# Row maxima of windowed attention in tiles of 64 queries of two heads by 320 keys

## The chip, the core and the metric

One Trainium2 chip, one core. The metric is device time in microseconds of one execution of the whole kernel. Engines are called PE (TensorE, matrix multiply; PEld is its weight load), DVE (VectorE), ACT (ScalarE), POOL (GpSimd) and SP (SyncE, which here only issues DMAs).

## What is computed

A transformer layer over 2048 tokens of width 512: layer norm, attention with 32 heads of 16 in a causal window of 256, a residual, a second layer norm, and a mixture of 8 experts of which each token takes two. The part that the change touches:

```python
scores = jnp.einsum("bhqd,bhkd->bhqk", q, k) * (Dh ** -0.5)
mask = (idx[:, None] - idx[None, :] >= 0) & (idx[:, None] - idx[None, :] < W)   # W = 256
scores = jnp.where(mask[None, None], scores, -1e9)
p = _softmax(scores, axis=-1)
o = jnp.einsum("bhqk,bhkd->bhqd", p, v)
```

## The kernel before

The tokens are worked in 4 chunks of 512 (`c`), the heads in 8 groups of 4 (`g`); a chunk and a group make a unit, 32 in all. `qk` (L583) projects Q and K of a unit in high and low halves of float32 (three matmuls for one product), writes them to DRAM (`qkd`) and reads them back into a slot of SBUF, of which there are four (`Q[i]`, `K[i]`, L263 to L266). In a slot, K holds two heads above each other: 48 rows from partition 0 are the 16 dimensions of an even head in three parts, 48 rows from partition 64 those of an odd head; its columns are 768 keys, 256 before the chunk and 512 of it. Q holds for each head only that head's rows; the others stay zero from a memset at the start (L477), so a matmul of a head's Q with the pair's K sees that head alone. `rq` (L631) and `rk` (L635) are the loads, one of each for the even heads and one for the odd ones; `rq` moves rows of 512 floats.

`maxes` (L647) finds each query's largest score. For a block of 128 queries and a head, one matmul (L666) has 128 queries as its weights and 384 keys as its moving operand; DVE adds a mask of the window to it and reduces it to the maximum in one instruction (L671, `tensor_tensor_reduce`, which the trace shows as CUSTOM_DVE_ANT_0 and a read of its accumulator). That is 16 matmuls and 16 reductions a unit. In chunk 0, where no keys lie before the first, blocks 0 and 1 have 128 and 256 keys, and several heads share a PSUM bank. At most three banks hold maxima (pool `mx`). `fin` (L677) negates and splits the maxima, a DMA writes them to DRAM (`md`, L684), and another (L687) reads them into rows 126 and 127 of the slot's Q, where K has ones. So the score matmuls of `attend` (L713), which have keys as weights and queries as moving operand, already subtract the maximum. ACT takes the exponential (L717), POOL clears what lies outside the window (L737), and PE multiplies by V (L758).

The order on every engine is made ahead by a planner: each step is given to `add` with an engine, a duration in ns and a priority, and `Plan.order` (L126) simulates them with pools of buffers (`one`: 7 PSUM banks; `qk`: 4 slots); a table `SHIFT` (L41) moves priorities of kinds of steps in spans of eight units. The engines then run exactly that order, and wait for each other by semaphores. Durations for a matmul are `n * 0.4355 + 8` (L215), for a reduction `110 + n * 1.041` (L675). From about 500 us on the experts run (`up` L1259, `down` L1290, `down_32` L1330).

## Time and profile before

| | us |
|---|---|
| median of 3 runs | 1072.37 |
| lowest and highest | 1070.73, 1073.33 |
| the profiled execution, device time | 1069.08 |
| its span in the trace | 1067.3 |

The page of the profile gives busy time by engine, the share of DMA engines, and groups of instructions by line. A busy PE counts from a matmul's start to its modelled end, and matmuls overlap, so the time that a matmul takes is read from the starts of a dense run of them. The granted clock of PE is 1.00, 2.4 GHz, in every stretch of attention.

### The profile page before, as it was taken

The page shows a single profiled execution, that of the slowest core. Times are in us where ns is not written, and L with a number is a line of the kernel's source. Part 1 is how long each engine was busy: PE and PEld are TensorE (multiplying, and loading weights), DVE is VectorE, ACT ScalarE, POOL GpSimd, SP SyncE. Part 2 cuts the span into 40 slices and gives each one's busy share as a digit, 9 for nine tenths or more (in the row PEclk, how much of TensorE's full clock was granted, in tenths as well). Part 3 has the DMA queues.
Part 4 walks back from the last instruction along what each step waited for, and adds up shares of the span by engine and source line. Part 5 has one row for each costly group of instructions (what it writes and reads, how often), then busy time and mean ns, then how long its engine had stood idle before and what let it go on. Part 6 is the DMA issues. An engine that isn't in the chain of part 4 may idle for free.

```text
span 1067.3 us, 19631 instructions
## 1 busy us (share of the span) xinstructions
PE 1037.5 (97%) x6722; PEld 862.7 (81%) x6722; DVE 673.9 (63%) x1834; ACT 540.0 (51%) x1139; POOL 610.8 (57%) x922
## 2 busy tenths in 40 slices
PE   9999999999999999998999999999999999999993
PEld 6777777877788777755889898999989998788893
DVE  9988888888787787884742645444564445645331
ACT  3376667565655766567624452552643624445230
POOL 6575569676786767688683161472853737542101
PEclk9999999999999999999999999999999999999997
DMA  7988978777784786864513644344634546354411
GB/s 248 235 250 214 227 194 247 194 178 197 188 246 125 170 244 168 237 182 148 174 43 97 160 126 112 84 105 116 154 94 100 126 123 151 99 143 133 109 35 26
DMA packets 102082, 165.57 MB, mean 155 GB/s; under 512 B 26052, under 2 KB 38404, under 8 KB 101972
## 3 DMA queue, kind: packets, MB, share of 16 engines
q1 hardware_dynamic: 87892, 146.48, 49.1%
q0 software_dynamic: 14080, 17.74, 9.8%
q8 instruction: 55, 0.90, 0.4%
q14 instruction: 55, 0.45, 0.1%
HBM read 111.91 MB, written 52.26 MB: 154 GB/s over the span
## 4 chain that ended last, share of the span: by engine, by line
PE 83%; DMA 5%; DVE 5%; POOL 3%; issue 1%; ACT 1%; SPq 1%; POOLq 0%; ACTq 0%; DVEq 0%
PE one L1259 24%; PE one L1290 15%; PE one L713 8%; PE one L666 8%; PE one L1330 7%; PE oT L758 7%; PE one L607 5%; PE one L836 3%; PE one L551 2%; PE one L927 1%; DVE one L671 1%; DMA mf<-in_A_wqk_dram 1%; DMA mf<-xnd,tb 1%; DMA mr<-md 1%; DMA mf<-in_A_x_dram 1%
## 5 line engine op out<-in xcount | busy, mean ns | idle before, releaser
L671 DVE CUSTOM_DVE_ANT_0 one<-one,masked 128x384 f32<-128x384 f32 (+2 forms) x512 | 260.7, 555 | 47.5 <-PE one L666 45.1
L1259 PE MATMUL one<-mr 128*128 128x288 f32 (+8 forms) x1716 | 266.4, 316 | 0.7 <-ACT mr L426 0.7
L1259 PEld LDWEIGHTS one<-mr 128*128 128x128 f32 (+1 forms) x1716 | 249.7, 186 | 12.9 <-ACT mr L426 0.9
L717 ACT ACTIVATE zone<-one 128x384 f32<-128x384 f32 (+1 forms) x480 | 207.0, 499 | 92.9 <-PE one L713 77.9
L737 POOL TENSOR_SCALAR_AFFINE_SELECT zone<-zone 128x256 f32<-128x256 f32 (+1 forms) x368 | 169.3, 483 | 90.4 <-ACT zone L717 88.6
L1290 PE MATMUL one<-zone,mr 128*128 128x512 f32 (+1 forms) x648 | 155.6, 396 | 0.0
L666 PE MATMUL one<-mr 126*128 126x384 f32 (+2 forms) x512 | 152.7, 350 | 1.7 <-DVE mx L671 1.7
L713 PE MATMUL one<-mr 128*128 128x384 f32 (+1 forms) x592 | 143.4, 316 | 2.7 <-DMA mr<-md 1.6
L1290 PEld LDWEIGHTS one<-zone,mr 128*128 128x128 f32 (+1 forms) x648 | 120.5, 187 | 29.0
L428 DVE TENSOR_TENSOR mr<-one,mr 128x512 fp32r<-128x512 f32 (+9 forms) x161 | 83.0, 526 | 89.3 <-ACT mr L426 89.0
L1311 POOL DMA_INDIRECT out_dram<-mf,tb x24 | 39.5, 1645 | 164.3 <-DVE mf L1301 153.3
L1198 POOL DMA_INDIRECT mf<-xnd,mf x97 | 103.2, 1063 | 43.9 <-issue 27.7
L430 POOL TENSOR_TENSOR mr<-mf,mr 128x512 fp32r<-128x512 f32 (+4 forms) x92 | 114.2, 1254 | 23.0 <-ACT mr L426 17.6
L426 ACT CAST mr<-mf 128x512 fp32r<-128x512 f32 (+6 forms) x148 | 108.9, 754 | 29.6 <-DMA mf<-in_A_wqk_dram 16.7
L666 PEld LDWEIGHTS one<-mr 126*128 126x128 f32 x512 | 89.5, 189 | 40.3 <-DVE mx L671 17.1
L1273 ACT ACTIVATE one<-one 128x288 f32<-128x288 f32 (+7 forms) x132 | 56.5, 428 | 128.1 <-PE one L1259 127.8
L713 PEld LDWEIGHTS one<-mr 128*128 128x128 f32 x592 | 102.1, 189 | 22.9 <-ACT zone L717 7.1
L1311 POOL DMA_INDIRECT out_dram<-mf x40 | 64.2, 1605 | 72.4 <-DVE mf L1340 62.8
L607 PE MATMUL one<-mr 128*128 128x512 f32 (+1 forms) x396 | 102.1, 387 | 0.9 <-DVE mx L671 0.9
L758 PE MATMUL oT<-zone 128*17 128x384 f32 (+2 forms) x1408 | 96.0, 387 | 2.4 <-POOL zone L737 2.4
L426 ACT CAST mr<-one 128x512 fp32r<-128x512 f32 (+9 forms) x161 | 73.4, 461 | 32.4 <-PE one L1232 20.2
L607 PEld LDWEIGHTS one<-mr 128*128 128x128 f32 x396 | 70.1, 188 | 11.6 <-DVE mx L671 1.3
(182 smaller groups left out, 1244.4 us busy)
## 6 DMA issues: line engine op xcount, KB each, us to landing
mf<-in_B_w_dram SPq DMA_DIRECT2D x32, 688.0 KB
mf<-in_B_w_dram SPq DMA_DIRECT2D x40, 512.0 KB
mr<-qkd SPq DMA_DIRECT2D x80, 192.0 KB
qkd<-mr SPq DMA_DIRECT2D x29, 512.0 KB
mr<-qkd SPq DMA_DIRECT2D x48, 288.0 KB
mf<-in_A_x_dram SPq DMA_DIRECT2D x32, 256.0 KB
mf<-in_A_wqk_dram SPq DMA_DIRECT2D x32, 256.0 KB
qkd<-mr SPq DMA_DIRECT2D x64, 128.0 KB
```

The costliest lines, as they stand in the source:

```text
L426: a = add("ACT", 51 + n * 0.86, lambda: nc.scalar.copy(dst_h(), src()), deps, prio, bufs)
L430: b = add("POOL", 60 + n * 2.3, lambda: nc.gpsimd.tensor_sub(dst_l(), src(), f32(dst_h())), [a], prio, bufs)
L607: nc.tensor.matmul(single[bk.h][:, s], wt()[:, int(i == 1), k * 128:(k + 1) * 128], xt[:, k, s], start=(i == 0 and k == 0), stop=(i == 2 a ...
L666: nc.tensor.matmul(view()[:, j], Q[slot.h][0:126, h + j, b * 128:(b + 1) * 128], K[slot.h][0:126, (h + j) // 2, (b + k0) * 128:(b + 3) * 1 ...
L671: nc.vector.tensor_tensor_reduce(v, v, masked.rearrange("p a k -> p (a k)")[:, 384 - n:], scale=1.0, scalar=NEG, op0=OP.add, op1=OP.max, a ...
L713: nc.tensor.matmul(single[bk.h][:, off:off + w], K[slot.h][:, h // 2, r * 128:(r + 1) * 128], Q[slot.h][:, h:h + hs, b * 128:(b + m) * 128 ...
L717: return add("ACT", 51 + n * 0.833, lambda: nc.scalar.activation(dst(), single[bk.h][:, 0:n].rearrange(order, q=128, **({"h": 2} if "h" in ...
L737: nc.gpsimd.affine_select(v, v, pattern=[[0, v.shape[1]], [-1 if far else 1, 128]], compare_op=OP.is_gt if far else OP.is_ge, fill=0.0, ba ...
L758: nc.tensor.matmul(oT[32 * j:32 * j + 17, b * 128:(b + n) * 128], V[blk % NV][:, 4 * g + j, :], PT[pt.h][j // 2][:, off:off + n, j % 2], s ...
L1259: nc.tensor.matmul(bank(), a[:, k, f * 128:f * 128 + w], spot[b][:, k, c0:c1], start=(i == 0), stop=(i == 11))
L1290: nc.tensor.matmul(single[bk.h][:n], h[a][:w], spot["w2"][2 * f + b][:w], start=(f == 0 and q == 0), stop=(f == NF - 1 and q == 2))
L1311: d = nc.gpsimd.indirect_dma_start(in_offset=None, compute_op=OP.add, **kw)
```

## The change

A tile of the maxima becomes 64 queries of two heads by 320 keys: the weights are 64 queries of an even head (which are zero in the odd head's rows) and the same 64 of the odd head, so its 128 rows are (head, query); 64 queries look at 64 + 256 keys. Eight blocks and two pairs of heads make 16 tiles a unit, as before. For the weights to lie together, Q is stored as (pair, block of 64, head of the pair, query). The loads of Q write in that layout, 64 floats at a time, and are issued by pair: four of 96 KB a unit in place of two of 192 KB. The score matmuls read Q in runs of 64. The mask is one row of 320 keys, the same in both halves of the partitions. In chunk 0 the first four blocks have 64, 128, 192 and 256 keys. The planner's durations follow from the sizes; `SHIFT` stays, and the names of the steps it speaks of keep their meaning (`rq`, whose name changes, has no entry).

```diff
--- before.py
+++ after.py
@@ -262,7 +262,7 @@
     R2 = at[id(mr)]
     Q, K = [], []
     for i in range(NQ):
-        Q.append(take(mr, 4, 512))
+        Q.append(take(mr, 2048))
         K.append(take(mr, 2, 768))
     R4 = at[id(mr)]
     woh, wol = take(mr, 4, 512), take(mr, 4, 512)
@@ -335,7 +335,7 @@
         return consts.tile(shape, dt, name=name)
 
     ident = const([128, 128], F32, "ident")
-    masked = const([128, 3, 128], BF, "masked")
+    masked = const([128, 320], BF, "masked")
     before = const([128, 128], BF, "before")
     ones = const([128, 128], BF, "ones")
     wgt = const([128, 4, E], F32, "wgt")
@@ -354,8 +354,8 @@
     ry_t = [const([128, 4], F32, f"ry{i}") for i in range(2)]
     v4_t = [const([128, 2], F32, f"v4{i}") for i in range(2)]
     h_t4 = [const([128, 2], F32, f"h4{i}") for i in range(2)]
-    mx_t = [const([128, 4, 4], F32, f"mx{i}") for i in range(NQ)]
-    mm_t = [const([128, 2, 4, 4], F32R, f"mm{i}") for i in range(NQ)]
+    mx_t = [const([128, 2, 8], F32, f"mx{i}") for i in range(NQ)]
+    mm_t = [const([128, 2, 2, 8], F32R, f"mm{i}") for i in range(NQ)]
     mt_t = [const([128, 32], F32, f"mt{i}") for i in range(NQ)]
     mv2_t = [const([128, 2], F32, f"mvh{i}") for i in range(NH)]
     ry2_t = [const([128, 1], F32, f"ryh{i}") for i in range(NH)]
@@ -391,9 +391,10 @@
 
     def consts_first():
 
-        nc.vector.tensor_scalar(masked[:, 0], jp_i, 0, NEG, op0=OP.is_le, op1=OP.mult)
-        nc.vector.memset(masked[:, 1], 0.0)
-        nc.vector.tensor_scalar(masked[:, 2], jp_i, 0, NEG, op0=OP.is_gt, op1=OP.mult)
+        nc.vector.memset(masked[:, 64:256], 0.0)
+        for r in (slice(0, 64), slice(64, 128)):
+            nc.vector.tensor_scalar(masked[r, 0:64], jp_i[r, r], 0, NEG, op0=OP.is_le, op1=OP.mult)
+            nc.vector.tensor_scalar(masked[r, 256:320], jp_i[r, r], 0, NEG, op0=OP.is_gt, op1=OP.mult)
         nc.vector.memset(oT, 0.0)
 
     def consts_dve():
@@ -628,19 +629,23 @@
         slots[u] = slot
         rds = []
         for par in range(2):
-            def rq(par=par):
-                nc.sync.dma_start(f32(Q[slot.h])[par * 64:par * 64 + 48, par::2],
-                                  ap(dd, par * 16 * 3 * S + o, [[S, 48], [32 * 3 * S, 2], [1, 512]]))
+            def rq(pr, par=par):
+                nc.sync.dma_start(f32(q_of(slot))[par * 64:par * 64 + 48, pr, :, par],
+                                  ap(dd, (2 * pr + par) * 16 * 3 * S + o, [[S, 48], [64, 8], [1, 64]]))
 
             def rk(par=par):
                 h = 256 if c else 0
                 nc.sync.dma_start(f32(K[slot.h])[par * 64:par * 64 + 48, :, 256 - h:768],
                                   ap(dd, 64 * 3 * S + S + par * 16 * 3 * S + o - h, [[S, 48], [32 * 3 * S, 2], [1, 512 + h]]))
             dep = wr + [m for k in range(min(u + 1, NQ)) for m in memsets[k]]
-            rds.append(dma(rq, 196608, dep, p + 0.6, [slot]))
+            rds.extend(dma(lambda pr=pr, rq=rq: rq(pr), 98304, dep, p + 0.6, [slot]) for pr in range(2))
             rds.append(dma(rk, 589824, dep, p + 0.6, [slot]))
         qk_read[u] = rds
     slots = {}
+
+    def q_of(slot):
+
+        return Q[slot.h].rearrange("p (a b e q) -> p a b e q", a=2, b=8, e=2)
     m_read = {}
     w_load = []
 
@@ -650,25 +655,25 @@
         slot = slots[u]
         box = {}
         reds = []
-        for b in range(4):
-            k0 = 0 if c else max(0, 2 - b)
-            n = (3 - k0) * 128
-            m = 512 // n
-            for h in range(0, 4, m):
+        for b in range(8):
+            k0 = 0 if c else max(0, 4 - b)
+            n = (5 - k0) * 64
+            m = min(2, 512 // n)
+            for h in range(0, 2, m):
                 bk, lim = Buf("one"), Buf("mx")
-                pp = p + b / 4 + h / 16
+                pp = p + b / 8 + h / 16
 
                 def view(n=n, m=m, bk=bk):
                     return single[bk.h][:, :m * n].rearrange("p (h n) -> p h n", h=m)
 
                 def mm(b=b, h=h, k0=k0, m=m, view=view):
                     for j in range(m):
-                        nc.tensor.matmul(view()[:, j], Q[slot.h][0:126, h + j, b * 128:(b + 1) * 128],
-                                         K[slot.h][0:126, (h + j) // 2, (b + k0) * 128:(b + 3) * 128], start=True, stop=True)
+                        nc.tensor.matmul(view()[:, j], q_of(slot)[0:126, h + j, b].rearrange("p e q -> p (e q)"),
+                                         K[slot.h][0:126, h + j, (b + k0) * 64:(b + 5) * 64], start=True, stop=True)
 
                 def red(j, b=b, h=h, n=n, view=view):
                     v = view()[:, j]
-                    nc.vector.tensor_tensor_reduce(v, v, masked.rearrange("p a k -> p (a k)")[:, 384 - n:], scale=1.0, scalar=NEG,
+                    nc.vector.tensor_tensor_reduce(v, v, masked[:, 320 - n:], scale=1.0, scalar=NEG,
                                                    op0=OP.add, op1=OP.max, accum_out=mx_t[slot.h][:, h + j, b:b + 1])
                 a = add("PE", m * max(107, mm_ns(n)), mm, qk_read[u], pp, [slot, bk, lim])
                 for j in range(m):
@@ -684,7 +689,7 @@
         w = dma(lambda: nc.sync.dma_start(box["d"], mt_t[slot.h]), 30000, [f], p + 1, [slot])
 
         def rd_():
-            nc.sync.dma_start(f32(Q[slot.h])[126:128].rearrange("p h (b i q) -> p (h b) i q", b=4, i=4),
+            nc.sync.dma_start(f32(Q[slot.h])[126:128].rearrange("p (b i q) -> p b i q", i=4, q=32),
                               ap(box["d"], 0, [[512, 2], [32, 16], [1024, 4], [1, 32]]))
         m_read[u] = [dma(rd_, 20000, [w], p + 1.1, [slot], 625)]
 
@@ -711,11 +716,11 @@
                     for r, b, m, h, hs in chunks:
                         w = m * hs * 128
                         nc.tensor.matmul(single[bk.h][:, off:off + w], K[slot.h][:, h // 2, r * 128:(r + 1) * 128],
-                                         Q[slot.h][:, h:h + hs, b * 128:(b + m) * 128], start=True, stop=True)
+                                         q_of(slot)[:, h // 2, 2 * b:2 * b + 2 * m, slice(None) if hs == 2 else h % 2], start=True, stop=True)
                         off += w
                 pe = add("PE", sum(mm_ns(m * hs * 128) + 2 for _, _, m, _, hs in chunks), mm, m_read[u] + qk_read[u], prio, [slot, bk, pt, lim])
                 return add("ACT", 51 + n * 0.833, lambda: nc.scalar.activation(
-                    dst(), single[bk.h][:, 0:n].rearrange(order, q=128, **({"h": 2} if "h" in order else {})), AF.Exp, scale=0.25),
+                    dst(), single[bk.h][:, 0:n].rearrange(order, **({"e": 2, "q": 64} if "e" in order else {"q": 128}), **({"h": 2} if "h" in order else {})), AF.Exp, scale=0.25),
                     [pe], prio, [bk, pt, lim])
 
             for pr in range(2):
@@ -725,7 +730,8 @@
                     k1, k2 = (2, 0) if name == "A" else (0, 1)
                     exps = [scores([(r2, b2, 2, h, 1), (r2, b2, 2, h + 1, 1)],
                                    lambda pt=pt, pr=pr, k2=k2: PT[pt.h][pr][:, k2:k2 + 2].rearrange("p b h q -> p h b q"), "p (h b q) -> p h b q", pp),
-                            scores([(r1, b1, 1, h, 2)], lambda pt=pt, pr=pr, k1=k1: PT[pt.h][pr][:, k1], "p (h q) -> p h q", pp + 1 / 16)]
+                            scores([(r1, b1, 1, h, 2)], lambda pt=pt, pr=pr, k1=k1: PT[pt.h][pr][:, k1].rearrange("p h (e q) -> p h e q", e=2),
+                                   "p (e h q) -> p h e q", pp + 1 / 16)]
                 else:
                     (r, b, _), = parts
                     exps = [scores([(r, b, 3, h + j, 1)], lambda pt=pt, pr=pr, j=j: PT[pt.h][pr][:, :, j], "p (b q) -> p b q", pp + j / 16) for j in range(2)]
```

The first place where the order changes is PE at the start of attention, in chunk 0 (`L607` and `L608` are the projection of Q and K, `L551` and `L552` that of V, `L666` and `L671` the maxima). Before:

```order
L551 MATMUL one_77<-mr 128x512 x4
L666 MATMUL one_78<-mr 128x128 x4
L666 MATMUL one_79<-mr 128x256 x2
L666 MATMUL one_80<-mr 128x256 x2
L607 MATMUL one_74<-mr 128x512 x8
L666 MATMUL one_75<-mr 128x384
L607 MATMUL one_74<-mr 128x512 x4
L666 MATMUL one_76<-mr 128x384
```

and now:

```order
L552 MATMUL one_77<-mr 128x512 x4
L608 MATMUL one_78<-mr 128x512 x4
L671 MATMUL one_79<-mr 128x64 x2
L671 MATMUL one_80<-mr 128x128 x2
L671 MATMUL one_74<-mr 128x192 x2
L608 MATMUL one_78<-mr 128x512 x4
L671 MATMUL one_75<-mr 128x256 x2
L608 MATMUL one_78<-mr 128x512 x4
L671 MATMUL one_76<-mr 128x320
L671 MATMUL one_79<-mr 128x320
```

The maxima of unit 0 now come one burst of the projection later, and in smaller pieces.

The second place is PE in a later chunk, with `L713` and `L718` the score matmuls and `L607` and `L608` the projection of a unit ahead. Before:

```order
L758 MATMUL oT<-zone 17x256 x4
L666 MATMUL one_77<-mr 128x384
L666 MATMUL one_76<-mr 128x384
L713 MATMUL one_74<-mr 128x384
L666 MATMUL one_79<-mr 128x384
L713 MATMUL one_75<-mr 128x384
L713 MATMUL one_80<-mr 128x384
L607 MATMUL one_78<-mr 128x512 x4
L666 MATMUL one_77<-mr 128x384
L666 MATMUL one_74<-mr 128x384
L713 MATMUL one_75<-mr 128x384
```

and now:

```order
L764 MATMUL oT<-zone 17x256 x4
L671 MATMUL one_78<-mr 128x320
L671 MATMUL one_79<-mr 128x320
L718 MATMUL one_80<-mr 128x384
L718 MATMUL one_76<-mr 128x384
L671 MATMUL one_75<-mr 128x320
L718 MATMUL one_74<-mr 128x384
L608 MATMUL one_77<-mr 128x512 x4
L671 MATMUL one_78<-mr 128x320
L671 MATMUL one_80<-mr 128x320
L718 MATMUL one_79<-mr 128x384
```

The mix is the same, one or two maxima to one or two score matmuls, in another rotation of the PSUM banks.

The third is SP's queue in chunk 0, around the maxima of unit 0 (`md` is written at `L684`, now `L689`, and read back at `L687`, now `L692`; `L632`, now `L633`, are loads of Q, `L637`, now `L638`, of K). Before:

```order
L621 DMA qkd_86<-mr 64x512
L622 DMA qkd_86<-mr 64x512
L684 DMA md_544<-mt_136 128x32
L620 DMA qkd_86<-mr 128x2x512
L591 DMA mf<-in_A_wqk_dram 128x512
L632 DMA mr<-qkd_85 48x2x512
L637 DMA mr<-qkd_85 48x2x512
L632 DMA mr<-qkd_85 48x2x512
L687 DMA mr<-md_544 2x64x32
L637 DMA mr<-qkd_85 48x2x512
L621 DMA qkd_87<-mr 64x512
```

and now:

```order
L622 DMA qkd_86<-mr 64x512
L592 DMA mf<-in_A_wqk_dram 128x512
L689 DMA md_551<-mt_136 128x32
L623 DMA qkd_86<-mr 64x512
L621 DMA qkd_86<-mr 128x2x512
L633 DMA mr<-qkd_85 48x8x64 x2
L638 DMA mr<-qkd_85 48x2x512
L692 DMA mr<-md_551 2x64x32
L633 DMA mr<-qkd_85 48x8x64 x2
L638 DMA mr<-qkd_85 48x2x512
```

The read-back has three loads of the next slot ahead of it in both; of the four loads of Q that replace two, two stand ahead of it.

## Rows read from the trace of the kernel before

**Rows 1.** The page, part 1: busy us of each engine, its share of the span, and its instructions.

```profile
PE 1037.5 (97%) x6722; PEld 862.7 (81%) x6722; DVE 673.9 (63%) x1834; ACT 540.0 (51%) x1139; POOL 610.8 (57%) x922
```

**Rows 2.** The page, part 4: the chain that ended last, its share of the span by engine and line.

```profile
PE one L1259 24%; PE one L1290 15%; PE one L713 8%; PE one L666 8%; PE one L1330 7%; PE oT L758 7%; PE one L607 5%; PE one L836 3%; PE one L551 2%; PE one L927 1%; DVE one L671 1%; DMA mf<-in_A_wqk_dram 1%; DMA mf<-xnd,tb 1%; DMA mr<-md 1%; DMA mf<-in_A_x_dram 1%
```

**Rows 3.** Busy time by stretch of the span: the stretch and its length in us, then busy us and number of instructions of PE, PEld, DVE, ACT and POOL, the granted clock, the DMA engines' share and GB/s.

```profile
25.00:75.00 50.00, 47.18 (x274) 37.40 (x273) 46.91 (x172) 25.06 (x53) 32.56 (x43) 1.00 0.93 250
75.00:125.00 50.00, 49.46 (x359) 35.08 (x358) 41.78 (x169) 34.63 (x78) 31.98 (x59) 1.00 0.90 223
125.00:225.00 100.00, 99.06 (x738) 77.42 (x740) 85.62 (x283) 61.35 (x136) 67.56 (x121) 1.00 0.80 206
225.00:325.00 100.00, 99.57 (x745) 78.41 (x734) 79.58 (x246) 61.77 (x138) 75.12 (x133) 1.00 0.78 207
325.00:475.00 150.00, 149.20 (x1153) 111.98 (x1153) 118.21 (x425) 97.99 (x219) 107.34 (x203) 1.00 0.70 185
475.00:555.00 80.00, 74.94 (x462) 58.10 (x462) 45.52 (x118) 44.23 (x98) 65.00 (x102) 1.00 0.39 120
```

**Rows 4.** Instructions of PE in order of time, from three places: attention at 376 us, the first expert at 538 us, a later expert at 726 us. Columns: start in us, length in us to the end of the last one, engine, line, operation, out<-in, shapes, number.

```profile
376.78 0.76 PE L713 MATMUL one<-mr 128*128 128x256 f32 x5
377.38 1.09 PE L607 MATMUL one<-mr 128*128 128x512 f32 x4
378.31 0.51 PE L666 MATMUL one<-mr 126*128 126x384 f32 x2
378.65 0.52 PE L713 MATMUL one<-mr 128*128 128x256 f32 x3
...
538.87 4.43 PE L1259 MATMUL one<-mr 128*128 128x384 f32 x24
543.15 0.18 PE L993 MATMUL one<-r_m,before 128*128 128x16 bf16 x1
...
726.45 4.12 PE L1330 MATMUL one<-mr,zone 128*128 128x320 f32 x27
730.40 1.05 PE L1330 MATMUL one<-mr 128*128 128x320 f32 x6
```

**Rows 5.** The same view of PE in chunk 0, between 40 and 60 us. The first row merges matmuls of 128, 256 and 384 columns and names the shape of the first. In brackets: idle time of the engine before the row, and what ended it.

```profile
40.86 1.08 PE L666 MATMUL one<-mr 126*128 126x128 f32 x8
41.78 2.90 PE L607 MATMUL one<-mr 128*128 128x512 f32 x12
...
53.00 0.76 PE L713 MATMUL one<-mr 128*128 128x384 f32 x3 [1.19 <-DMA mr<-md]
```

**Rows 6.** Groups of instructions by line and shape over the whole span: number, then busy us, mean ns of one, and idle us of the engine before them with what ended it.

```profile
L671 DVE CUSTOM_DVE_ANT_0 one<-one,masked 128x384 f32<-128x384 f32 x448 | 239.2, 582 | 45.4 <-PE one L666 44.1
...
L671 DVE CUSTOM_DVE_ANT_0 one<-one,masked 128x256 f32<-128x256 f32 x32 | 13.7, 446 | 0.5
...
L671 DVE CUSTOM_DVE_ANT_0 one<-one,masked 128x128 f32<-128x128 f32 x32 | 9.5, 297 | 1.6 <-PE one L666 0.9
```

**Rows 7.** Who waited for whom from 0 to 475 us: us in total, times, the longest in us. PEld is PE's weight load.

```profile
PEld one L666 <- DVE mx L671: 16.9, 32, 1.1
...
PEld one L713 <- DVE mx L671: 4.2, 8, 0.6
...
PE one L666 <- DVE mx L671: 1.7, 4, 0.8
```

**Rows 8.** DMA packets of SP's queue (q1) in five stretches, one row each: 132 to 133 us (all 93 packets hold under 512 B; 128 B each by their bytes), 391.5 to 392 us (81 packets under 2 KB; 80 of them of 1 KB), 653.5 to 656.5 us (475 packets, 454 of 2 KB or more), 25 to 125 us, and 125 to 475 us. Columns: packets, MB, share of 16 engines' time in the stretch.

```profile
q1 hardware_dynamic: 93, 0.01, 7.5%
...
q1 hardware_dynamic: 81, 0.08, 45.9%
...
q1 hardware_dynamic: 475, 0.93, 90.5%
...
q1 hardware_dynamic: 15447, 23.51, 91.1%
...
q1 hardware_dynamic: 45267, 68.50, 74.1%
```

**Rows 9.** The chain of waits that ends at 60 us, in order of time: start in us, length in us, what. SPq is SP's issue of a DMA.

```profile
47.10 0.58 SPq L632
...
47.78 5.09 DMA mr<-md
```

**Rows 10.** Two issues of a Q load on SP in order of time, columns as in rows 4.

```profile
22.67 0.37 SPq L632 DMA_DIRECT2D mr<-qkd  x1
...
23.58 0.44 SPq L632 DMA_DIRECT2D mr<-qkd  x1
```

**Rows 11.** DVE's two mask constants, and the first and the last of GpSimd's (POOL) memsets beside them, columns as in rows 4.

```profile
22.13 4.64 DVE L394 TENSOR_SCALAR masked<-mf 128x128 bf16<-128x128 int32 x1
22.22 1.40 POOL L478 MEMSET mr<- 128x1536 f32 x1
...
22.34 4.50 DVE L396 TENSOR_SCALAR masked<-mf 128x128 bf16<-128x128 int32 x1
...
25.30 1.40 POOL L478 MEMSET mr<- 128x1536 f32 x1
```

**Rows 12.** Reductions of DVE in chunk 0 in order of time, the first and the last of six, columns as in rows 4.

```profile
46.37 0.60 DVE L671 CUSTOM_DVE_ANT_0 one<-one,masked 128x384 f32<-128x384 f32 x1
...
48.94 0.60 DVE L671 CUSTOM_DVE_ANT_0 one<-one,masked 128x384 f32<-128x384 f32 x1
```

## The prediction

> **What bounds the kernel now.** I read the share of busy time by engine first, then stretches of the span. TensorE (PE) is busy 97% of the span and nothing else is over 81% [rows 1]; in the chain that ended last the maxima's matmuls (L666) are 8% and the score matmuls (L713) 8% [rows 2]. The stretches show where the change can act: attention runs from about 25 to 475 us, and there PE is busy 47.2 of 50, 49.5 of 50, 99.1 of 100, 99.6 of 100 and 149.2 of 150 us; from 555 us on PE works for the experts, which the change leaves alone [rows 3]. In the first 50 us of attention two other things are nearly full as well: VectorE (DVE) is busy 46.9 of 50 us, and the DMA engines have a share of 0.93 [rows 3].
>
> A busy PE is not yet a PE at its rate, since matmuls overlap in the record. So I take a matmul's price from the starts of dense runs. Five score matmuls of 256 columns start in 0.60 us (376.78 to 377.38), 120 ns each; two maxima's matmuls of 384 columns start in 0.34 us (378.31 to 378.65); 24 expert matmuls of 384 columns take 4.28 us to the next kind (538.87 to 543.15), 178 ns each; four of 512 columns take 0.93 us (377.38 to 378.31), 233 ns each; 27 of 320 columns take 3.95 us (726.45 to 730.40), 146 ns each [rows 4]. Price follows columns. For 384 I take 176 ns, half way between 256 and 512, which lies between the two direct readings of 170 and 178.
>
> **The change part by part.**
>
> *Matmuls of the maxima.* Their number stays: 16 a unit, 32 units. In the 24 units of chunks 1 to 3 all 384 go from 384 to 320 columns: 384 x (176 - 146) = 11.5 us of PE. In the 8 units of chunk 0, eight a unit do the same: 64 x 30 = 1.9 us. The other eight there go from 128 and 256 columns to 64, 128, 192 and 256. Eight of the old ones take 0.92 us (40.86 to 41.78, 115 ns each) [rows 5], hardly less than 256 columns alone, so I take nothing for these; by columns alone it would be up to 0.9 us more. Sum 13.4 us off PE's own work, on the path, because PE is what attention waits for.
>
> *Reductions on DVE (L671).* They last 582, 446 and 297 ns for 384, 256 and 128 columns [rows 6], 1.06 ns a column at the upper end, so 320 columns save 68 ns: 384 x 68 = 26.1 us. In chunk 0 a unit goes from 4 x 297 + 4 x 446 + 8 x 582 = 7.63 us to about 6.79 (222, 297, 372 and 446 twice each, 514 eight times): 8 x 0.84 = 6.7 us. Together 32.8 us less of DVE. DVE is off the path over most of attention; what counts is where PE waits for it. Up to 475 us the weight loads of PE wait 16.9 us ahead of L666 and 4.2 us ahead of L713 for a reduction, 40 times [rows 7], 0.53 us on average. Three maxima may be in flight, so at most 3 x 68 = 0.20 us of each wait goes, some 8 us in all; weight loads run ahead of matmuls, and the matmuls themselves stood idle for a reduction only 1.7 us [rows 7]. The ends are 0 and 21.1 us; I take 4 us.
>
> *Loads of Q.* Each of the two loads a unit becomes two, and rows of 2 KB are written as eight pieces of 256 B: 4 x 48 x 8 = 1536 packets a unit for 192. The trace has no 256 B packet from this queue. Its neighbours: 93 packets of 128 B take 7.5% of 16 engines in 1 us, 12.9 ns each; 81 of 1 KB take 45.9% in 0.5 us, 45.3 ns; 475, nearly all 2 KB, take 90.5% in 3 us, 91.5 ns [rows 8]. On the line between the first two, 256 B cost 17.5 ns, the value I take, since 128 B is the nearest; the ends are 12.9 and 45.3 ns. Old: 192 x 91.5 / 16 = 1.10 us of all engines a unit. New: 1536 x 17.5 / 16 = 1.68 us. So 0.58 us more a unit, 18.6 us over 32 units. From 125 to 475 us queue 1 holds 74.1% [rows 8]; 14 us more there lies beside PE's work. From 25 to 125 us it holds 91.1% [rows 8]; 8 x 0.58 = 4.6 us more fits into the 8.9 us left, but loads will queue longer, and one wait for a transfer shows already: the scores of unit 0 wait 1.19 us at 53.00 for the maxima's row written back into Q, read by a DMA that stands behind waiting loads of Q and K [rows 5, 9]. I take 2 us; ends 0 and 17.
>
> The Trainium skill speaks against this load: in "DMA: Bandwidth & Descriptors", Specifications, it asks for at least 512 B a transfer, since below that the engine does a read-modify-write. By that rule, taken as a doubling of the line's price, a piece would cost 35 ns, and the sum would change by the first 9 us of rival two. The 128 B packets here, 12.9 ns apiece [rows 8], do not show it.
>
> *The sync queue (SP).* 64 more issues of Q loads; such an issue lasts 0.37 to 0.44 us [rows 10], so 0.9 us more a unit. A unit takes some 14 us (32 units in 450), with about ten DMAs of its own at such a price, so SP has room. In front of the maxima's read-back of unit 0 stand three loads, as before, in the new order too. Nothing.
>
> *Reading Q for the scores.* A 256-column operand is now four runs of 64, a 384-column one six; the two-head form becomes one piece. Of the five matmuls at 376.78 one reads two runs of 128, the other four one run, and the five still start 120 ns apart [rows 4], so a break costs nothing that shows. I take 0. The upper end: 512 columns at 233 ns and 256 at 120 leave 7 ns a matmul that columns do not explain; if each extra run cost that, 256 x 5 + 224 x 3 - 112 = 1840 runs would cost 13 us. A gain has no reason here.
>
> *Mask constants and order.* Two mask writes become four of a quarter's size, and one memset grows. Today both end at 26.8 us, after 4.64 and 4.50 us, with GpSimd memsets running from 22.22 to 26.70 [rows 11]; whatever holds them there will hold the new ones. Nothing, at most 0.4 us. The planner orders everything anew from shorter durations, while its table of shifts stays; the shown places keep their pattern. I take 1 us lost, ends -4 and +8.
>
> Sum: -13.4 - 4 + 2 + 1 = -14.4 us. The profiled execution took 1069.08 us, so 1054.7; the median of the three runs lies 3.29 us above it, and I carry that: **1058 us**.
>
> **Rivals.** *One: PE's saving turns into waiting.* If ScalarE's exponentials or GpSimd's masks set the pace, fewer columns buy idle time, and 0 to 3 us remain: about 1071. Against it: ACT and POOL are busy 61 to 75 of 100 us in 125 to 325 us [rows 3]. For it: the short stretch from 475 us, where PE is busy 74.9 of 80. If runs of 64 slow PE's reads, the 13 us above eat the gain with the same result. Together 0.11.
>
> *Two, slower: the Q pieces make DMA the bound.* The place is 25 to 125 us. Its 8.9 us of room for 8 units are used up at 2.21 us a unit, 23 ns a piece. Beyond, each unit's Q comes late and PE stands. At twice the taken price, 35 ns: 8 x (3.36 - 1.10) - 8.9 = 9.2 us lost there against 11.5 won in later chunks, about 1070. At 45.3 ns, the price of a 1 KB packet: 8 x (4.35 - 1.10) - 8.9 = 17.1 lost, net +5.6: about 1078. It turns slower by over 0.3% from 42 ns. For it: the share of 0.93 and queued reads; against it: 12.9 ns for 128 B. Chance of 35 ns or more 0.12, two thirds of it slower.
>
> *Three: the new order is bad.* The table's shifts were made for longer maxima; a wait of 1 us in every other unit would cost 16 us and leave about 1074. Against it: the pattern in PE's and SP's rows stays. Chance 0.06.
>
> *Four: DVE was the real bound of the maxima.* Then all 21.1 us of waiting go too: 1072.37 - 13.4 - 21.1 + 3 = 1041. For it: from 46.37 to 48.94 us six reductions start 0.51 us apart, back to back [rows 12]. Chance 0.08.
>
> **How the numbers follow.** The forecast has 0.63 and its own range is 1050 to 1066. A measurement of this kernel can tell 0.3%, 3.2 us, from no change. Faster: the forecast, rival four and a little of rival one, 0.75. Within 0.3%: most of rival one and the 35 ns case, 0.11. Slower: the rest of rival two, rival three, 0.14. The range is 1045 to 1074: below it is most of rival four, above it the dear half of rival two.
>
> **What would show it.** Right: the maxima's matmuls of 320 columns start 146 ns apart in dense runs, reductions of about 514 ns, score matmuls unchanged at 120 and 176 ns, experts starting 12 to 17 us earlier, DMA share in the first 100 us of attention about 0.95, packets under 512 B up by 49,152 to some 75,000, each near 17 ns. Wrong: waits of the maxima's or the scores' matmuls for loads of Q, weight loads waiting for DMA ahead of the first maxima of a unit, a share of 1 in chunk 0, or a PE that is idle between attention and experts for longer than before.

## The result and the profile after

The changed kernel is slower: 1079.75 us median of 11 runs (1075.61 to 1081.32) against 1070.93 us for the kernel before on the same chip (1068.37 to 1075.14, 11 runs), a ratio of 1.0068, 95% interval 1.0055 to 1.0081. The forecast was 1058 us with a range of 1045 to 1074. The profiled execution took 1081.0 us, its span 1079.3.

The page of the changed kernel, part 1 (columns as in [rows 1]), its line of DMA packets, and queue 1 (packets, MB, share of 16 engines' span):

```profile
PE 1041.7 (97%) x6722; PEld 857.5 (79%) x6722; DVE 640.9 (59%) x1836; ACT 540.2 (50%) x1139; POOL 611.4 (57%) x922
...
DMA packets 146114, 165.58 MB, mean 153 GB/s; under 512 B 76228, under 2 KB 88580, under 8 KB 146004
...
q1 hardware_dynamic: 131924, 146.48, 48.6%
```

The two DMA lines of the page before:

```profile
DMA packets 102082, 165.57 MB, mean 155 GB/s; under 512 B 26052, under 2 KB 38404, under 8 KB 101972
...
q1 hardware_dynamic: 87892, 146.48, 49.1%
```

The work changed as forecast: DVE is busy 33.0 us less (forecast 32.8), and 50,176 more packets are under 512 B (forecast 49,152; the other 1,024 come with the 64 more DMAs, for e2 below has them without a piece of 256 B). The stretches, columns as in [rows 3]:

```profile
25.00:75.00 50.00, 45.28 (x248) 33.62 (x247) 40.36 (x163) 23.97 (x48) 31.27 (x42) 1.00 0.97 245
75.00:125.00 50.00, 49.78 (x356) 35.46 (x355) 40.24 (x174) 33.73 (x76) 32.00 (x58) 0.97 0.77 194
125.00:225.00 100.00, 98.84 (x727) 75.64 (x727) 74.96 (x264) 61.12 (x136) 66.82 (x117) 1.00 0.87 218
225.00:325.00 100.00, 94.65 (x692) 71.96 (x691) 68.45 (x245) 60.65 (x135) 72.41 (x128) 0.97 0.73 189
325.00:475.00 150.00, 148.89 (x1161) 111.70 (x1159) 107.68 (x411) 93.50 (x212) 102.95 (x194) 1.00 0.71 197
```

Against [rows 3] PE is busy 1.90 us less from 25 to 75 us and 4.92 us less from 225 to 325 us, and executes fewer matmuls there (248 for 274, 692 for 745); elsewhere it is as full as before. Yet from 125 to 225 us it executes 727 matmuls for 738, though the maxima's are shorter, so a full PE is not a PE at its rate there either. The granted clock, 1.00 throughout before, is 0.97 in two stretches. So PE did not run ahead with its shorter work: it stood, and now and then ran slowly. PE in order of time at the two widest gaps and in a dense run (columns as in [rows 4], in brackets the idle time ahead and what ended it):

```profile
71.24 0.96 PE L764 MATMUL oT<-zone 128*17 128x384 f32 x8
74.09 0.90 PE L671 MATMUL one<-mr 126*128 126x64 f32 x6 [1.89 <-DMA od<-zone]
...
259.55 0.41 PE L671 MATMUL one<-mr 126*128 126x320 f32 x1
262.06 0.44 PE L718 MATMUL one<-mr 128*128 128x384 f32 x1 [2.10 <-DVE mx L676]
...
264.73 0.47 PE L671 MATMUL one<-mr 126*128 126x320 f32 x1
265.00 0.52 PE L718 MATMUL one<-mr 128*128 128x384 f32 x1
...
381.80 0.69 PE L718 MATMUL one<-mr 128*128 128x384 f32 x3
382.32 1.09 PE L608 MATMUL one<-mr 128*128 128x512 f32 x4
383.25 0.46 PE L671 MATMUL one<-mr 126*128 126x320 f32 x2
383.54 0.34 PE L718 MATMUL one<-mr 128*128 128x384 f32 x1
```

At 383 us two maxima of 320 columns start in 0.29 us, 145 ns each (forecast 146): the price of the columns was right. Three scores of 384 columns start in 0.52 us (381.80 to 382.32), 173 ns each, so the runs of 64 that they now read cost nothing that shows, as forecast. After the matmul of 259.55 PE waits for a reduction. What held the reduction stands on DVE:

```profile
256.13 0.50 DVE L676 CUSTOM_DVE_ANT_0 one<-one,masked 128x320 f32<-128x320 f32 x1 [0.40 <-PE one L671]
...
260.61 0.95 DVE L803 RECIPROCAL r<-r 96x128 f32<-96x128 f32 x1 [3.92 <-DMA r<-od]
261.48 0.47 DVE L676 CUSTOM_DVE_ANT_0 one<-one,masked 128x320 f32<-128x320 f32 x1
```

The planner put the reciprocal of chunk 1 ahead of the reductions. It needs a DMA that SP issued at 256.52 us; DVE executes in order, so the reductions behind it stood 3.92 us, and PE behind them 2.10 us. Then the clock fell, as two short stretches behind that place show (the eighth figure is the granted clock):

```profile
263.60:266.90 3.30, 3.30 (x11) 2.94 (x10) 2.25 (x10) 1.56 (x5) 1.53 (x4) 0.50 0.91 190
267.00:270.00 3.00, 3.00 (x34) 1.80 (x32) 1.95 (x8) 1.58 (x4) 1.45 (x4) 1.00 1.05 358
```

At 0.50 (1.2 GHz) a maxima's matmul takes 0.27 us (264.73 to 265.00). Who waited for whom from 0 to 475 us, as [rows 7]:

```profile
PEld one L671 <- DVE mx L676: 12.7, 30, 0.8
...
PEld one L718 <- DVE mx L676: 9.6, 14, 2.3
DVE r L803 <- DMA r<-od: 5.6, 2, 3.9
PE one L718 <- DVE mx L676: 4.1, 4, 2.1
```

The waits of the maxima's weight loads fell from 16.9 to 12.7 us, which is the 4 us forecast, but those of the scores' rose from 4.2 to 9.6, and the longest from 0.6 to 2.3 us: the waits moved, they did not go.

As a measure of attention I use one event: ScalarE's copy of the result of attention's last unit. Before:

```profile
504.27 0.59 ACT L773 COPY zone<-oT 128x512 f32<-128x512 f32 x1 [2.93 <-PE oT L758]
```

After:

```profile
518.44 0.59 ACT L779 COPY zone<-oT 128x512 f32<-128x512 f32 x1 [1.99 <-PE oT L764]
```

It comes 14.2 us later, where the forecast had the experts start 12 to 17 us earlier. (A second profiled execution, e5, has it at 513.33: single executions of one kernel differ here by some 5 us.)

### The profile page after: what moved, and what is told of

Read it like the earlier page. It is cut to its first block, busy times and chain, and to the rows that moved or that the text cites. A ratio compares the mean times of both kernels' runs of the same rounds, so it can differ in the third digit from the quotient of the medians.

```text
span 1079.3 us, 19705 instructions
## 1 busy us (share of the span) xinstructions
PE 1041.7 (97%) x6722; PEld 857.5 (79%) x6722; DVE 640.9 (59%) x1836; ACT 540.2 (50%) x1139; POOL 611.4 (57%) x922
## 2 busy tenths in 40 slices
DMA packets 146114, 165.58 MB, mean 153 GB/s; under 512 B 76228, under 2 KB 88580, under 8 KB 146004
## 4 chain that ended last, share of the span: by engine, by line
PE 79%; DMA 7%; POOL 4%; DVE 4%; SPq 2%; issue 2%; ACT 1%; ACTq 0%; DVEq 0%; POOLq 0%
PE one L1265 23%; PE one L1296 15%; PE one L1336 7%; PE one L718 7%; PE oT L764 6%; PE one L608 6%; PE one L671 6%; PE one L842 3%; PE one L552 2%; DMA mr<-qkd 2%; POOL zone L743 1%; DMA qkd<-mr 1%; PE one L933 1%; POOL table L1030 1%; DMA od<-zone 1%
## 5 line engine op out<-in xcount | busy, mean ns | idle before, releaser
L676 DVE CUSTOM_DVE_ANT_0 one<-one,masked 128x320 f32<-128x320 f32 (+4 forms) x512 | 228.7, 494 | 79.4 <-PE one L671 77.4
L718 PE MATMUL one<-mr 128*128 128x384 f32 (+1 forms) x592 | 148.0, 326 | 9.1 <-DVE mx L676 4.1
L671 PE MATMUL one<-mr 126*128 126x320 f32 (+4 forms) x512 | 140.2, 327 | 4.3 <-DMA od<-zone 1.9
L718 PEld LDWEIGHTS one<-mr 128*128 128x128 f32 x592 | 99.9, 192 | 38.7 <-DVE mx L676 10.1
L1204 POOL DMA_INDIRECT mf<-xnd,mf x97 | 102.8, 1060 | 43.7 <-issue 27.4
L671 PEld LDWEIGHTS one<-mr 126*128 126x128 f32 x512 | 90.4, 191 | 39.6 <-DVE mx L676 14.4
L608 PE MATMUL one<-mr 128*128 128x512 f32 (+1 forms) x396 | 102.7, 389 | 0.4 <-POOL mr L431 0.3
L764 PE MATMUL oT<-zone 128*17 128x384 f32 (+2 forms) x1408 | 101.0, 394 | 0.1
L427 ACT CAST zone<-mf 128x512 fp32r<-128x512 f32 x72 | 42.0, 620 | 73.4 <-PE one L1336 54.8
```

The lines of the kernel that those rows point to most:

```text
L427: a = add("ACT", 51 + n * 0.86, lambda: nc.scalar.copy(dst_h(), src()), deps, prio, bufs)
L608: nc.tensor.matmul(single[bk.h][:, s], wt()[:, int(i == 1), k * 128:(k + 1) * 128], xt[:, k, s], start=(i == 0 and k == 0), stop=(i == 2 a ...
L671: nc.tensor.matmul(view()[:, j], q_of(slot)[0:126, h + j, b].rearrange("p e q -> p (e q)"), K[slot.h][0:126, h + j, (b + k0) * 64:(b + 5) ...
L676: nc.vector.tensor_tensor_reduce(v, v, masked[:, 320 - n:], scale=1.0, scalar=NEG, op0=OP.add, op1=OP.max, accum_out=mx_t[slot.h][:, h + j ...
L718: nc.tensor.matmul(single[bk.h][:, off:off + w], K[slot.h][:, h // 2, r * 128:(r + 1) * 128], q_of(slot)[:, h // 2, 2 * b:2 * b + 2 * m, s ...
L764: nc.tensor.matmul(oT[32 * j:32 * j + 17, b * 128:(b + n) * 128], V[blk % NV][:, 4 * g + j, :], PT[pt.h][j // 2][:, off:off + n, j % 2], s ...
```

## The experiments

Eighteen runs (e5 is the change once more, e18 is e1). The first four ran on a chip on which every kernel took some 60 us longer in the experts' part, so from it only ratios and attention are used. Medians and ratios to the kernel before on the same chip, with their 95% intervals:

| run | work, order | us | ratio |
|---|---|---|---|
| e1 | change's, order of before | 1129.09 | 0.9986 (0.9966 to 1.0005) |
| e18 | the same, another chip | 1071.30 | 0.9996 (0.9978 to 1.0013) |
| e2 | before's, Q loads issued in four | 1134.14 | 1.0035 (1.0016 to 1.0055) |
| e3 | before's, order of the change | 1151.57 | 1.0195 (1.0167 to 1.0222) |
| e4 | as e3, runs of 64 floats | 1151.88 | 1.0192 (1.0164 to 1.0220) |
| e5 | the change again | 1080.37 | 1.0078 (1.0055 to 1.0102) |
| e6 | change's, no shifts | 1099.37 | 1.0260 (1.0237 to 1.0284) |
| e7 | before's, no shifts | 1103.61 | 1.0314 (1.0291 to 1.0337) |
| e8 | change's, told 336 for 320 | 1086.65 | 1.0149 (1.0131 to 1.0166) |
| e11 | change's, told 304 | 1089.61 | 1.0173 (1.0147 to 1.0198) |
| e12 | change's, told 368 | 1081.51 | 1.0096 (1.0077 to 1.0116) |
| e9 | the change, three moves by hand | 1078.98 | 1.0079 (1.0058 to 1.0100) |
| e10 | e18, three moves by hand | 1073.87 | 1.0020 (1.0005 to 1.0035) |
| e13 | the change, Q in 2 KB rows | 1147.05 | 1.0703 (1.0684 to 1.0722) |
| e17 | e18, Q in 2 KB rows | 1133.79 | 1.0568 (1.0537 to 1.0598) |
| e14 | before, half the rows | 1246.57 | 1.1635 (1.1616 to 1.1653) |
| e15 | e18, half the rows | 1237.95 | 1.1562 (1.1539 to 1.1585) |
| e16 | the change, half the rows | 1254.52 | 1.1706 (1.1683 to 1.1729) |

**Work and order taken apart.** The theory ORDER says that the new order of the instructions costs the time, the rival PIECES that the 256 B loads do. e1 puts the change's tiles into before's order on every engine, by grouping chunk 0's tiles as before and telling the planner before's lengths:

```diff
+        groups = ... [[(0, 0), (0, 1), (1, 0), (1, 1)]] + [[(b, 0), (b, 1)] for b in (2, 3)] + ...
+            was = {4: 128, 2: 256, 1: 384}[len(group)]
-                a = add("PE", m * max(107, mm_ns(n)), mm, ...
+            a = add("PE", len(group) * max(107, mm_ns(was)), mm, ...
```

> The changed kernel, but the planner is told the sizes of before, so that every engine runs exactly the order of before (SP with the extra Q loads in the places of the old ones). Theory ORDER (the plan made anew is what costs: about 13 us of columns won, some 20 lost in new waits and in the low clock that follows them): about 1058 us, 13 below before. Theory PIECES (Q loads of 256 B cost, whatever the order): as the change, 1078 to 1082 us.

0.9986: ORDER's direction, but 0.14% where it expected over 1%. e2 takes before and issues each Q load as two, written as runs of 64 floats:

```diff
-  nc.sync.dma_start(f32(Q[slot.h])[par * 64:par * 64 + 48, par::2], ap(dd, ..., [[S, 48], [32 * 3 * S, 2], [1, 512]]))
+  for pr in range(2):
+      nc.sync.dma_start(f32(Q[slot.h])[..., 2 * pr + par].rearrange("p (b q) -> p b q", q=64), ap(dd, ..., [[S, 48], [64, 8], [1, 64]]))
```

> The kernel before with its order, its layout and its 384-column tiles; only each Q load is issued as two DMAs that move 64 floats at a time (1536 packets of 256 B a unit for 192 of 2 KB). ORDER: 1071 to 1074 us, within 0.3% of before. PIECES: 1085 to 1092 us, since 13 us of columns are not won and the loss of the change stays.

1.0035, about 4 us (2 to 6 by the interval), but not a test of pieces. Its line of DMA packets:

```profile
DMA packets 103106, 165.58 MB, mean 147 GB/s; under 512 B 27076, under 2 KB 39428, under 8 KB 102996
```

Runs that lie side by side at both ends were joined to 2 KB packets again (27,076 under 512 B, not 76,000); only the doubled issues are left in it. They are not free. The reciprocal near 250 us, which in before held DVE up for 1.03 us, now holds it for 3.97, and PE behind it for 2.34 us; at 252.73 us the granted clock falls to 0.50 for 3.41 us:

```profile
249.85 0.95 DVE L798 RECIPROCAL r<-r 96x128 f32<-96x128 f32 x1 [3.97 <-DMA r<-od]
...
251.37 0.44 PE L714 MATMUL one<-mr 128*128 128x384 f32 x1 [2.34 <-DVE mx L672]
```

e3 has before's tiles of 384 columns in the change's order (the planner is told the change's lengths; Q in four loads of 2 KB rows); e4 is the same with runs of 64 floats, which were joined too:

```diff
+                now = (5 - (0 if c else max(0, 4 - 2 * b - h // 2))) * 64
-                a = add("PE", m * max(107, mm_ns(n)), mm, ...
+                a = add("PE", m * max(107, mm_ns(now)), mm, ...
```

> The kernel before with its 384-column tiles and its layout, in exactly the order of the change on every engine; Q loads are four of 96 KB a unit but of 2 KB rows. ORDER: 1088 to 1094 us, some 20 above before. PIECES: 1069 to 1074 us, like before.

> The third kernel of this set with Q loads in pieces of 64 floats: the order and the loads of the change, the tiles of before. The change less this run is what 320 columns give in the new order. ORDER: 1088 to 1094 us, as the run with whole rows, and the columns are worth 10 to 14 us. PIECES: 1085 to 1092 us and 10 to 14 us above the run with whole rows. If columns are worth nothing (a third theory, that PE never was the bound): 1078 to 1082 us.

1.0195 and 1.0192: two measurements of one kernel, 0.3 us apart, where ORDER expected them. With not one column changed, the new order and its 64 more issues cost 20 us; over e2, which has the issues alone, the order costs 17.4 us (1134.14 to 1151.57). And the change stands 1.27% (1.0195 to 1.0068) under e3, some 13.6 us, with about 3 us to either side by the intervals: in the new order the new work brings about what was forecast for its columns.

**Is it this order, or any that is new?** FITTED says that the table of shifts suits before's order alone, ONE ORDER that the change's order is an unlucky one. e6 and e7 are the change and the kernel before with `SHIFT = {}`, e5 the change again.

> The change as it is, beside the next three on one chip. Both theories: 1.0055 to 1.0081 of the kernel before, with the five stretches of clock 0.5 at about 11, 76, 229, 264 and 496 us of attention, since the order is the same. If the ratio is under 1.002 or over 1.012, chips differ by more than the intervals say, and small ratios from different chips can't be set side by side.

> The change, planned with an empty table of shifts. Theory FITTED (the table's numbers were right for the old order only, and with the change they move tasks at random): without the table the change keeps its time, 1.00 to 1.01 of before, and is at least 10 us better than the kernel before without the table. Theory ONE ORDER (the table still helps; this order happens to hold some bad waits): without the table the change loses as much as the kernel before does without it, 1.02 or more.

> The kernel before, planned with an empty table of shifts. FITTED: the table is worth about what the new order lost, so 1.015 to 1.025 (some 20 us), with PE gaps of 1 to 3 us on DVE mx and on DMA and clock 0.5 behind them. ONE ORDER: under 1.008, for then the order matters little in general and the change's order is an exception.

e5 repeats the ratio, but not the five stretches of low clock that were expected with it: between 25 and 500 us it has two, at 442.8 and 487.2 us. The table is worth 31.7 us to the kernel before (1103.61 to 1071.86), and 19.0 to the change (1099.37 to 1080.37). FITTED's price for before is met and passed; its claim that the table does nothing for the change is wrong: 13 of 32 us of its worth are lost, not all. Without it on either side the change is 4.2 us the faster. e8, e11 and e12 only tell the planner other lengths for the maxima and reductions (e8: `mm_ns(n * 21 // 20)`, e11 19/20, e12 23/20):

> The change's work, but the planner is told 336 columns for each maxima and reduction of 320 (and the same factor, 1.05, for the shorter ones), so that tasks fall in another order. ONE ORDER: some orders are good; this one misses most of the named waits (PE gaps over 0.9 us at 71.7, 226, 241, 259, 492) and gives 0.988 to 1.000. FITTED: any order but the fitted one holds as many waits elsewhere, with two to six stretches of clock 0.5 before the experts, and gives 1.003 to 1.012.

> The change's work, the planner told 0.95 of the columns (304 for 320). A third order of the same instructions. FITTED (any order to which the table wasn't fitted costs alike): 1.003 to 1.018, as the two known orders (1.007 and 1.015), with 8 to 17 us of idle time over 0.9 us and low clock before the experts. ONE ORDER: under 1.000.

> The same with 1.15 of the columns told (368 for 320), near what the planner was told before (384). FITTED: if the table is tied to the told lengths, this one lies nearer to before than the others, 0.993 to 1.005; if it is tied to the exact order, 1.003 to 1.018 as for the other orders. ONE ORDER: under 1.000.

Three more orders of the same instructions, none faster than the change's own: 1.0096 to 1.0173, of which the lowest (e12) is not clear of e5's 1.0078. All three lie far over the 1.000 of ONE ORDER, which falls; e8 lies over the range of FITTED too, and e12 gives what FITTED expected if the table is tied to the exact order. In none of five orders that were not before's is this work faster than the kernel before; in before's it is level with it.

**Can the named waits be taken away one at a time?** NAMED WAITS says that the loss is made of single waits, SLACK that an early PE waits at the next thing. e9 and e10 move three instructions in the finished order and nothing else (e10: 2 tasks for the route):

```diff
+MOVES = (('inverse.DVE1', 0, 2), ('inverse.DVE1', 2, 4), ('route.s3.PE', 0, 3))
-    order = plan.order()
+    order = moved(plan.order(), plan.tasks)
```

> The change with three instructions moved by hand in the finished order, all else as planned: the reciprocals at 138 and 254 us go behind 2 and 4 more reductions on VectorE, the route's matmuls at 224 us behind 3 more tasks on TensorE. Theory NAMED WAITS (the loss is made of single waits, each worth its length and the clock that falls behind it): the gaps of 1.64 us at 254 and 1.66 us at 222 go, and with them up to 3.4 us of low clock, so 3 to 7 us less than the change, 1.001 to 1.005 of before. Rival SLACK (TensorE then stands at the next instruction that comes late): the same time as the change, 1.006 to 1.009, with new gaps of over 0.9 us within 10 us behind the old places.

> The change's work in the old order (0.9986 of before), with the same three instructions moved (2 and 4 reductions, 2 tasks of TensorE). NAMED WAITS: the gap of 2.34 us at 252 (DVE mx, behind a reciprocal that waited 4.0 us for DMA r<-od), the clock 0.5 behind it and the 0.99 us at 224 go: 3 to 6 us less, 0.993 to 0.996 of before, and so a version faster than both. SLACK: 0.997 to 1.000.

Nothing is won (1.0079; 1.0020, even 2.6 us over e18). PE of e9, at the old place of the gap and behind it:

```profile
255.42 0.41 PE L671 MATMUL one<-mr 126*128 126x320 f32 x1
255.67 0.34 PE L718 MATMUL one<-mr 128*128 128x384 f32 x1
...
261.85 0.50 PE L718 MATMUL one<-mr 128*128 128x256 f32 x2
264.41 0.38 PE L671 MATMUL one<-mr 126*128 126x320 f32 x1 [2.05 <-DMA mr<-qkd]
```

The wait for DVE is gone from 255.42, and 9 us on the next unit's maxima stand 2.05 us for their loads. PE of e10:

```profile
256.51 0.50 PE L724 MATMUL one<-mr 128*128 128x256 f32 x2
259.30 0.39 PE L676 MATMUL one<-mr 126*128 126x320 f32 x1 [2.29 <-DMA qkd<-mr]
...
274.98 1.09 PE L608 MATMUL one<-mr 128*128 128x512 f32 x4
278.26 0.42 PE L676 MATMUL one<-mr 126*128 126x320 f32 x1 [2.18 <-DVE mx L682]
```

2.34 us saved, 2.29 and 2.18 met later. NAMED WAITS falls; SLACK stands, though e10 lies a little over its range as well: a PE that is early waits at the next thing.

**What does the early PE wait for?** For bytes in flight, says LOADS; for fixed latencies and hand-offs, says ROUND TRIPS. e14, e15 and e16 load 24 of each 48 rows of Q and K (`[S, 48]` becomes `[S, 24]`). e13 and, later, e17 load whole rows of Q as one run of 512 floats, so bytes and DMAs stay and the pieces go, while queries lie in wrong places:

```diff
-  f32(q_of(slot))[par * 64:par * 64 + 48, pr, :, par], ap(dd, ..., [[S, 48], [64, 8], [1, 64]])
+  f32(Q[slot.h])[par * 64:par * 64 + 48, (2 * pr + par) * 512:][:, 0:512], ap(dd, ..., [[S, 48], [1, 512]])
```

Other values mean other routing, and the experts get more work: part 1 of the page counts 6834 matmuls in e13 and e17, 7058 in e14 to e16, 6722 else. So only runs of one such group are compared with each other, and attention, which does the same work in all.

> The change in its own order, its Q loads with the same bytes and the same number of DMAs, but each row as one run of 512 floats (2 KB packets) and not 8 pieces of 64 floats; the queries then lie in the wrong places of the tile, nothing else is touched. PIECES (the 256-byte packets slow the loads, and the waits of the change come from that): 0.997 to 1.002 of before. ORDER (they cost the DMA engines nothing that anything waits for): 1.005 to 1.009, as the change, with packets under 512 B back at some 26,000.

> The kernel before, with 24 of each 48 rows of Q and K loaded (half the bytes and packets of these loads; the other rows keep their first values). LOADS (time off TensorE waits for bytes in flight): its own time falls little, 0.995 to 1.000, for TensorE is the bound in its order; ROUND TRIPS (fixed latencies and hand-offs): 0.997 to 1.001.

> The change's work in the old order, with 24 of each 48 rows loaded. LOADS: the columns' saving comes out, 11 us or more under the kernel before with half rows, 0.984 to 0.991 of before. ROUND TRIPS: as with whole rows, at most 5 us under it, 0.993 to 1.000.

> The change in its own order, with 24 of each 48 rows loaded. LOADS: the waits of the new order are loads that come late, so 0.990 to 1.001 of before. ROUND TRIPS, and waits for DVE, ACT and POOL that an order out of step brings: 1.002 to 1.008, still slower than before.

I had not reckoned with the experts, so the ratios expected there say nothing; the differences do. The copy of the last unit's result in e14, the kernel before with half the rows:

```profile
505.21 0.59 ACT L773 COPY zone<-oT 128x512 f32<-128x512 f32 x1 [2.92 <-PE oT L758]
```

In e15, the change's work in the old order with half the rows:

```profile
493.79 0.59 ACT L785 COPY zone<-oT 128x512 f32<-128x512 f32 x1 [2.91 <-PE oT L770]
```

Half the loads bring the kernel before nothing (505.21 against 504.27): PE was its bound. The change's work in the old order gains 11.4 us on it, and 8.6 us on the whole run (1237.95 against 1246.57), between the 11 that LOADS asked for and the 5 that ROUND TRIPS allowed: there the larger part of the columns' saving comes out. In the change's own order (e16) the copy is at 511.82, and the run 8.0 us slower than e14: there LOADS is wrong, and the new order's loss stays, whatever is loaded. Nor do 2 KB rows help it: e13 has its copy at 517.07, inside the two of the change (513.33 and 518.44).

> The change's work in the old order, each row of Q loaded as one run of 512 floats (2 KB packets), so that the queries lie in the wrong places; bytes and number of DMAs as in the change. PIECES (the 256-byte packets eat the gain in the old order): the last unit's result is copied at 492 to 498 us, 6 us or more before the kernel before (504), and the run is 1.05 to 1.058 of before, 13 us or more under the change with 2 KB rows (1.0703, which has the same wrong values and so the same work for the experts). BYTES (the loads' bytes as a whole): the copy at 502 to 508 us, the run 1.06 to 1.067.

> The change's work in the old order once more, on the chip of the run above. PIECES and BYTES alike: 0.997 to 1.003 of before, the last unit's result copied at 504 to 508 us, with TensorE gaps over 0.8 us on DMA (mr<-md, mr<-qkd, qkd<-mr) in unit 0 to 5 and around 250.

The copy in e17:

```profile
500.59 0.59 ACT L785 COPY zone<-oT 128x512 f32<-128x512 f32 x1 [2.93 <-PE oT L770]
```

In e18, the same order with pieces:

```profile
509.13 0.59 ACT L785 COPY zone<-oT 128x512 f32<-128x512 f32 x1 [2.94 <-PE oT L770]
```

So in the old order the pieces cost 8.5 us by these two executions (7.1 by that of e1, the program of e18 on another chip, whose copy is at 507.69). That is the larger part of the 15.3 between e18 and e15. Of the other 6.8, between e17 and e15, 4.9 are idle time of PE: its gaps of over 0.15 us between 20 us and that copy sum to 13.1 us in e17 (4.8 of them ended by a DMA) and to 8.2 in e15 (2.5), against 8.3 (1.6) before. 500.59 lies just under the range expected for BYTES and over that for PIECES; the run (13.3 us under e13) is what PIECES gave. e18 has the ratio that was expected, and its copy 1.1 us over the range. Where the 8.5 us lie is seen at two places. PE of e17:

```profile
50.92 0.40 PE L676 MATMUL one<-mr 126*128 126x256 f32 x2
52.81 0.76 PE L724 MATMUL one<-mr 128*128 128x384 f32 x3 [1.49 <-DMA mr<-md]
...
245.35 0.31 PE L676 MATMUL one<-mr 126*128 126x320 f32 x1
246.83 0.44 PE L724 MATMUL one<-mr 128*128 128x384 f32 x1 [1.17 <-DVE mx L682]
```

PE of e18:

```profile
51.24 0.40 PE L676 MATMUL one<-mr 126*128 126x256 f32 x2
54.15 1.30 PE L724 MATMUL one<-mr 128*128 128x384 f32 x3 [2.50 <-DMA mr<-md]
...
252.32 0.31 PE L676 MATMUL one<-mr 126*128 126x320 f32 x1
255.44 0.69 PE L724 MATMUL one<-mr 128*128 128x384 f32 x1 [2.81 <-DVE mx L682]
```

At both places a small DMA takes longer, from its issue on SP to the end of the wait: the maxima's row 5.44 us in e18 and 4.95 in e17, the input of the reciprocal 5.57 and 4.28. For the latter DVE stands 4.52 us in e18 and 2.87 in e17. And in e18 the clock falls at both, from 53.34 and 254.72 us while PE still stands, for 6.83 us each; a stretch of the second:

```profile
255.00:261.00 6.00, 5.55 (x16) 5.00 (x17) 4.26 (x18) 2.46 (x5) 1.69 (x5) 0.50 1.07 200
```

In e17 the clock stays at 1.00 through all of attention. The first unit's copy is 4.1 us later in e18 than in e17 (67.5 to 63.4), unit 8's 5.0 (160.0 to 155.0), unit 16's 8.7 (290.2 to 281.5), the last 8.5: most of the loss is these two places. PE's longer gaps there are 1.0 and 1.6 us of it; most of the rest is two times 6.83 us at half the clock, up to 3.4 us lost in each.

That the pieces delay these DMAs is not shown. For the maxima's row the times with pieces are 5.44, 5.36 and 4.99 us (e18, e1, and e10, which up to 138 us is the same program), without them 4.95, 5.18 and 5.22 (e17, e2, before). For the reciprocal's input they are 5.57 and 5.35 (e18, e1) against 4.28, 5.09 and 4.07, and PE stands 2.34 us in e2 as in e1, so there the doubled issues may do most of it. What a gap costs hangs on the clock: in e10 PE's first gap is 1.62 us, the clock stays, and the first unit's copy is at 64.7 us, 1.3 behind e17's and not 4.1.

## Why the prediction was wrong

*Matmuls of the maxima, -13.4 us, "on the path".* The size was right (145 ns a matmul; some 13.6 us between e3 and the change), but "on the path" held only in part. In before's order without the pieces, though with the doubled issues, the copy comes 3.7 us earlier (504.27 to 500.59), with half the loads 11.4 us earlier. Before the change PE was at once the bound and in step with its loads; 13 us faster, it reaches data that have not landed (PE's gaps ended by a DMA are 4.8 us in e17, 1.6 before). That is rival one, which I had placed with ScalarE and GpSimd; the runs place it with the loads.

*DVE, -4 us.* DVE's own 33 us are right, and so is the fall of 4.2 us in the wait I looked at. The wait beside it rose by 5.4 us.

*SP, the strided reads and the masks, 0 us.* The reads cost nothing that shows; SP was not free: e2, with 64 more issues and nothing else, took some 4 us more, where the step said nothing.

*Loads of Q, +2 us, ends 0 and 17.* The price of a piece was nearly right. From the start to some 18 us behind the last unit's copy queue 1 works these shares of 16 engines' time, first in e17 (0 to 518 us), then in e18 (0 to 528 us):

```profile
q1 hardware_dynamic: 68717, 104.23, 73.6%
```

```profile
q1 hardware_dynamic: 111906, 104.60, 77.4%
```

0.774 x 528 - 0.736 x 518 = 27.4 us more, against the 18.6 I reckoned. With 91.5 ns for each of the 6144 packets of 2 KB that went [rows 8], a piece costs (27.4 + 6144 x 0.0915 / 16) x 16 / 49,152 = 20 ns, for 17.5 taken. The pieces themselves stand in e18's trace: up to the copy the median of the 49,152 is 18 ns, their mean 24. The medians on this queue, 13, 18, 27, 46 and 84 ns for 128 B, 256 B, 512 B, 1 KB and 2 KB, lie on one line, 8 ns and 1 ns more for every 27 B. The Trainium skill's rule of 512 B in "DMA: Bandwidth & Descriptors", Specifications, taken as a doubling to 35 ns: these runs do not show it. What the step missed is who waits. I asked whether the pieces fit into the room that the engines have; they do, but at two places all of PE waits for a small DMA, and in e18 and e1 the clock falls in the gap or right behind it. Cost in the old order 7 to 8.5 us by single executions; in the change's order none that shows (e13).

*Order, +1 us, ends -4 and +8.* This step failed: 1 us was taken for the order, and the runs show 8 to 17. The new order costs 17.4 us with before's work (e3 against e2), 13.3 us with the change's work and 2 KB rows (e13 against e17), 8.4 us with the pieces (1079.75 against 1071.30); in the last two PE has loads to wait for in either order. I judged by looking: the shown places kept their pattern. But the order was fitted to the lengths, with a table worth 31.7 us, and no few rows show that. Rival three named the mechanism, with a price of 16 us and a chance of 0.06.

By the copy of the last unit, one execution each: 504.27 before, -3.7 for the new work in the old order with 2 KB rows, +8.5 for the pieces, +9.3 for the order, 518.44. Single executions of one kernel differ by some 5 us, so no term is surer than that. What follows the copy takes 560.8 to 563.0 us in before, e5, e18 and the change, so executions differ ahead of it; carried from each profiled execution to the median of its kernel, I estimate -6.8, +8.3 and +9.6. Nor do the terms keep their size in another sequence: with the order first, e13 has no pieces and its copy is as late as the change's (517.07 against 513.33 and 518.44). So the order alone is enough to make the change slower, while the pieces and the issues alone eat up what the work wins (e18). No version that was run beats the kernel before beyond its interval (e1 0.9986, e18 0.9996).

*Still open.* The copy comes 14.2 us later, and by the forecast's columns it should come 13.4 earlier. From the gaps and the low clock of the change I can name about half of these 27.6 us. Four stretches of low clock between 75 and 500 us (at 75.8, 229.4, 263.5 and 495.6, of 3.41 us each, about 1.7 us lost in each) are 7 us, and PE's record holds 7.0 us more idle time from 25 to 475 us. The rest hides where the record shows PE busy: from 20 us to the copy, without gaps of over 0.15 us and with the time at half the clock counted half, PE takes 476 us before and 476 after, with 13 us less to do. The score matmuls, whose size is unchanged, take most more of it (97.8 to 102.6 us from start to start). That it is made of short waits ahead of weight loads is likely, but I did not assign them one by one, and it is not shown. Nor is it shown why the input of the reciprocal takes longer in e2. Not tried: the change's tiles with a table of shifts fitted to them anew, which is what these runs point to.
